# One-token attention and mixer layers on one core: query products spread over four row groups of PSUM, and unread products in the tail's pauses

## The chip, the core and the metric

The kernel runs on one core of a Trainium2 chip. The metric is device time in microseconds of one execution, lower is better. Engines are named as in the profile: PE is TensorE (its weight loads are listed apart as PEld), DVE is VectorE, ACT is ScalarE, POOL is GpSimd, and SP is the engine whose queue issues nearly all DMA transfers.

## The reference

Two requests (B = 2), each with one new token of width D = 512, go through four blocks: attention, mixer, attention, mixer, with the same weights for both layers. Everything is float32.

```
x = x + attention(layernorm(x), k_cache, v_cache, wq, wo)
x = x + mixer(layernorm(x), w1, b1, w2, b2)
x = x + attention(layernorm(x), k_cache, v_cache, wq, wo)
x = x + mixer(layernorm(x), w1, b1, w2, b2)

attention: 32 query heads of 128, 8 cache heads (4 query heads share one),
           32768 cached positions; softmax(q k^T / sqrt(128)) v, then @ wo
mixer:     u = gelu_tanh(h * w1 + b1)  (512 channels x 1792 hidden), y = u @ w2 + b2
```

Each layer has to read both caches (2 x 8 x 32768 x 128 values each), and layer 1's query needs the whole of layer 0. Some parts of the caches that layer 0 has read last are kept in SBUF for layer 1.

## The kernel before

**Units and steps.** The work is cut into 32 *units* (layer, request b, cache head h). A unit has 64 K cells and 64 V cells; a cell is 128 partitions x 512 floats (256 KB). `Order` writes out by hand one list of *steps*, each of four cells of one unit's K or V; the list sets the order of everything. A K step (`k_step`, L330) multiplies four cells by the unit's query into four different groups of 32 partitions of one PSUM bank. A V step (`v_step`, L383) multiplies four cells by the exponentials, also into four partition groups, of `acc`. Units alternate: the K of the next unit, then the V of this one. Steps 992 to 1007 are the V of the last unit but one, 1008 to 1023 the V of the last unit, whose last eight cells (a "thin" block, L392) use smaller products into a tile of `rows`.

**Memory and loads.** `mem` holds 106 cells. `plan_loads` goes through the steps in order and decides for each load its size, its place in `mem`, and after which step it is released, which is the last step that uses the cells it overwrites. To choose among places and sizes it keeps an estimate of when the DMA queue and TensorE are where; what a step's hooks cost TensorE comes from the `us=` figures given to `at`, summed in `busy`. SP issues the loads in that order (L790), each waiting until its cells are free.

**Hooks.** All other work is attached to steps with `at(step, function, ...)` and runs right after that step in program order:

- `make_q` makes queries, for both requests at once where it can. Its parts are hooked at three steps: two of the four products of `xn` (normalised input, 128 x 4 parts x 2 requests) with `wq` (L293), the other two and a copy to a row in SBUF (L298), and four small products that turn the row into columns (L302), which `q_out` copies into `qz` (L316).
- `take_out` copies `acc` (L414), `out_sum`/`out_1` add up its parts (L422), `out_2` applies `wo` (L446) and accumulates in `rows`.
- At the end of layer 0 of a request, `mix_1`, `mix_2`, `half_way` and `hidden_tiles` (L502, L517) compute the mixer while the V of a *filling* unit of the other request goes on, four cells a load. Then `change_1` and `change_2` make layer 1's first query: `columns` turns the mixer's output into four columns (L546), L558 adds the residual to give the new `x`, and L562 multiplies the raw `x`, and a column of ones beside it, by `wq` while mean and variance are found with `all_sum` (L540); the two results are combined with `pair` (L581).
- For the last unit, `last_rows` and `last_mixer` compute the last mixer with nothing left to load: sums (L422, L432), `wo` (L619), the row spread over all partitions (L628), statistics, fourteen hidden tiles on ScalarE (L662, L673) and their products (L652), and the store (L680).

The four accumulating products of a query (L293, L562) all write the same one or two PSUM rows:

```
for d in range(step * DT // 2, (step + 1) * DT // 2):
    nc.tensor.matmul(
        q_ps[us][:n, :], xn[layer][:, d, b : b + n], wq[:, d, :], start=(d == 0), stop=(d == DT - 1)
    )
```

Of the kernel before, what the change touches and what calls it, by code (L numbers as in the profile page):

```python
# [8 lines left out]
F32 = mybir.dt.float32  # L9
AF = mybir.ActivationFunctionType  # L10
ALU = mybir.AluOpType
# [184 lines left out]
def gqa_mixer_kernel(ctx: ExitStack, tc: tile.TileContext, x, kt, v, wqo, cols, out):  # L196
# [39 lines left out]
    acc = pfix.tile([P, G], F32, name="acc")  # L236
    rows = [pfix.tile([P, G], F32, name=f"rows{b}") for b in range(B)]
    S = [const.tile([P, G], F32, name=f"S{k}") for k in range(2)]
    xn = [const.tile([P, DT, B], F32, name=f"xn{k}") for k in range(2)]
    xq = [const.tile([P, DT, 2], F32, name=f"xq{b}") for b in range(B)]  # L240
    xT = {}

    def constants():
        make_identity(nc, ident)
        nc.gpsimd.memset(one, 1.0)
        nc.gpsimd.memset(half_neg, -0.5)
        nc.gpsimd.memset(qz, 0.0)
        for t in xq:
            nc.gpsimd.memset(t, 1.0)
        nc.vector.tensor_reduce(  # L250
            selg, ident.rearrange("p (g r) -> p r g", g=NG)[:, : R * QT, :], axis=AX.X, op=ALU.add
        )
        nc.vector.memset(acc, 0.0)
        for t in rows:
            nc.vector.memset(t, 0.0)

    def first_input():
        cen = work.tile([P, B, DT], F32, name="cen", bufs=1)
        sq = work.tile([P, B, DT], F32, name="sq", bufs=1)
        m = work.tile([P, B], F32, name="x_m", bufs=1)  # L260
        rs = work.tile([P, B], F32, name="x_rs", bufs=1)
        p = pmisc.tile([P, G], F32, name="misc")
        nc.tensor.matmul(p[:, : B * DT], ones, xcols.rearrange("p b d -> p (b d)"), start=True, stop=True)
        nc.vector.tensor_reduce(m, p[:, : B * DT].rearrange("p (b d) -> p b d", b=B), axis=AX.X, op=ALU.add)
        nc.vector.tensor_scalar_mul(m, m, 1.0 / D)
        for b in range(B):
            nc.vector.tensor_scalar_sub(cen[:, b, :], xcols[:, b, :], m[:, b : b + 1])
        nc.vector.tensor_mul(sq, cen, cen)
        p = pmisc.tile([P, G], F32, name="misc")
        nc.tensor.matmul(p[:, : B * DT], ones, sq.rearrange("p b d -> p (b d)"), start=True, stop=True)  # L270
        nc.vector.tensor_reduce(rs, p[:, : B * DT].rearrange("p (b d) -> p b d", b=B), axis=AX.X, op=ALU.add)
        nc.vector.tensor_scalar(rs, rs, 1.0 / D, EPS, op0=ALU.mult, op1=ALU.add)
        nc.gpsimd.tensor_tensor(rs, rs, half_neg.to_broadcast([P, B]), op=ALU.pow)
        for b in range(B):
            xT[b] = xcols[:, b, :]
            nc.vector.tensor_scalar_mul(xn[0][:, :, b], cen[:, b, :], rs[:, b : b + 1])

    def row_tile():
        return work.tile([P, D], F32, name="row", bufs=1)
# [4 lines left out]
    def make_q(us, step):  # L284

        layer, b, h = us[0]
        n = len(us)
        wq = wq_sb[layer, h] if (layer, h) in wq_sb else wq_sb[0, h]
        if step == 0:
            q_ps[us] = pmisc.tile([P, G], F32, name="misc")  # L290
        if step < 2:
            for d in range(step * DT // 2, (step + 1) * DT // 2):
                nc.tensor.matmul(  # L293
                    q_ps[us][:n, :], xn[layer][:, d, b : b + n], wq[:, d, :], start=(d == 0), stop=(d == DT - 1)
                )
        if step == 1:
            q_row[us] = row_tile()
            nc.vector.tensor_copy(q_row[us][:n, :], q_ps[us][:n, :])  # L298
        if step == 2:
            pt = pmisc.tile([P, G], F32, name="misc")  # L300
            for r in range(R):
                nc.tensor.matmul(  # L302
                    pt[:, r * n : (r + 1) * n],
                    q_row[us][:n, r * DH : (r + 1) * DH],
                    ident[:n, :n],
                    start=True,
                    stop=True,
                )
            q_out(us, pt)

    def q_out(us, pt):
        n = len(us)
        for j, u in enumerate(us):
            q_at[u] = 28 + 32 * (turn[0] % SLOTS)
            turn[0] += 1
            nc.vector.tensor_copy(  # L316
                qz[:, q_at[u] : q_at[u] + R], pt[:, : n * R].rearrange("p (r b) -> p b r", b=n)[:, j, :]
            )
# [214 lines left out]
    negm = const.tile([P, 1], F32, name="negm")  # L533
    spread = const.tile([P, 1], F32, name="spread")
    sq = const.tile([P, DT], F32, name="sq")
    pair = const.tile([2, 1], F32, name="pair")

    def all_sum(dst, src):
        p = pmisc.tile([P, G], F32, name="misc")
# [13 lines left out]

    def change_1(key, y):
        b = key[1]
        x = xq[b][:, :, 0]
        wq = wq_sb[0, y[2]]
        nc.vector.tensor_add(x, columns(key), sq)  # L558
        xT[b] = x
        q_ps[y] = pfix.tile([P, G], F32, name="bcast")  # L560
        for d in range(DT):
            nc.tensor.matmul(q_ps[y][:2, :], xq[b][:, d, :], wq[:, d, :], start=(d == 0), stop=(d == DT - 1))  # L562
        all_sum(negm, x)
        nc.vector.tensor_scalar_mul(negm, negm, -1.0 / D)
        nc.vector.tensor_scalar_add(xn[1][:, :, b], x, negm)
        nc.vector.tensor_mul(sq, xn[1][:, :, b], xn[1][:, :, b])
        q_row[y] = row_tile()
        nc.scalar.activation(q_row[y][:2, :], q_ps[y][:2, :], AF.Copy)

    def change_2(key, y):  # L570
        b = key[1]
        all_sum(spread, sq)
        nc.vector.tensor_scalar(spread, spread, 1.0 / D, EPS, op0=ALU.mult, op1=ALU.add)
        nc.gpsimd.tensor_tensor(spread, spread, half_neg, op=ALU.pow)
        nc.vector.scalar_tensor_tensor(
            pair, ident[:2, 1:2], negm[:2, :], ident[:2, 0:1], op0=ALU.mult, op1=ALU.add
        )
        nc.vector.tensor_scalar_mul(pair, pair, spread[:2, :])
        pt = pmisc.tile([P, G], F32, name="misc")
        for r in range(R):  # L580
            nc.tensor.matmul(  # L581
                pt[:, r : r + 1], q_row[y][:2, r * DH : (r + 1) * DH], pair, start=True, stop=True
            )
        q_out((y,), pt)
        nc.vector.tensor_scalar_mul(xn[1][:, :, b], xn[1][:, :, b], spread)

    rest = [None, None]

    def last_rows(u):
        layer, b, h = u  # L590
# [13 lines left out]
    def last_mixer(u):  # L604
# [12 lines left out]
        for k in range(2):  # L617
            for r in range(R):
                nc.tensor.matmul(  # L619
                    rest[k][32 * r : 32 * r + 1, :w],  # L620
                    oT[u][:, r : r + 1],
                    wo_of(u)[:, r, k * w : (k + 1) * w],
                    start=True,
                    stop=True,
                )
        nc.vector.tensor_copy(y[:, :w], rest[0][:, :w])
        nc.scalar.activation(y[:, w:], rest[1][:, :w], AF.Copy)
        nc.tensor.matmul(p, sel1, y, start=False, stop=True, skip_group_check=True)  # L628
# [2 lines left out]
        for g in range(NG):  # L631
            nc.tensor.matmul(
                rows[b][32 * g : 32 * g + 1, :P],
                selg[:, 0:1],
                y[:, g * P : (g + 1) * P],
                start=False,
                stop=False,
                skip_group_check=True,
            )
        nc.vector.bn_aggr(mv, st)  # L640
        deviation(rs, mv)
        off = work.tile([P, 1], F32, name="off", bufs=1)
# [18 lines left out]
        for f in range(DIRECT):  # L661
            nc.scalar.activation(  # L662
                tiles[f], flat, AF.Gelu_apprx_tanh, bias=bias[:, f : f + 1], scale=scale[:, f : f + 1]
            )
            project_last(f)
        f0 = DIRECT
        for m in TAIL_GROUPS:
            for f in range(f0, f0 + m):
                nc.vector.tensor_scalar(
                    tiles[f], flat, scale[:, f : f + 1], bias[:, f : f + 1], op0=ALU.mult, op1=ALU.add  # L670
                )
            t = cells(tail_at + f0, m)
            nc.scalar.activation(t, t, AF.Gelu_apprx_tanh)  # L673
            for f in range(f0, f0 + m):
                project_last(f)
            f0 += m
        assert f0 == FT
        o = tiles[FT][:, :P]
# [7 lines left out]
        busy[p] = busy.get(p, 0.0) + us  # L686

    def queries(us, p0, p1, p2):
        at(p0, make_q, us, 0, us=1.3)
        at(p1, make_q, us, 1, us=1.3)  # L690
        at(p2, make_q, us, 2, us=1.0)

    changed = {y: (x, fill) for x, fill, y in order.changes}
    opening = order.units[0]
# [21 lines left out]
    for u in order.units:  # L716
# [18 lines left out]
        if u == order.last:  # L735
            at(v0 - 1, take_rows, key)
            at(v0 - 1, table, AF.Gelu_apprx_tanh)
            at(v0 - 1, mix_1, key)
            at(v0 - 1, last_rows, u)
            at(v_end - 2, take_out, u)  # L740
            at(v_end - 1, out_sum, u)
            at(v_end, last_mixer, u)
            continue
# [21 lines left out]
            at(e + 1, mix_4, key, us=1.2)  # L765
            continue
        (y,) = [y for y, (x, _) in changed.items() if x == u]
        at(e + 1, change_1, key, y, us=2.8)
        at(e + 2, change_2, key, y, us=0.8)
        assert e + 2 < first["K", y]  # L770

# [85 lines left out]
```

## Time and profile before

| | |
|---|---|
| median of 3 runs | 2518.88 us (2519.59, 2512.27, 2518.88) |
| the profiled execution: time / span | 2518.04 / 2516.3 us |
| busy: PE, PEld, DVE, ACT, POOL | 1430.8, 400.0, 181.2, 186.2, 5.0 us |
| HBM read | 1064.33 MB, 423 GB/s over the span |
| mean granted PE clock | 0.754 |

Instructions are listed by the line that records them. A matmul in float32 shows as two records, and a group of them as one row with a count. "idle <-X" is the time for which the engine waited before them, and what ended that wait. The clock column of a window is the share of full TensorE speed that was granted; the DMA share is the mean over the core's 16 DMA engines. In a timeline, a row is start, duration, engine, line, operation, tiles, count; rows of equal kind may be merged, so a row's duration can hold waits inside it.

### The profile page before, as it was taken

The numbers are of one execution on the slowest core, as the hardware profiler recorded it, in microseconds if no ns is written. First come the engines' busy times: TensorE is split into PE (matmuls) and PEld (weight loads), VectorE is DVE, ScalarE is ACT, GpSimd is POOL, SyncE is SP. The second block draws the span as 40 slices with busy tenths as digits, with TensorE's granted clock in tenths as the row PEclk, the third lists the DMA queues.
The fourth block names the chain that finished last, engine by engine and source line by source line (L and its number), as shares of the span: only waits on it lengthen the run. The fifth ranks groups of instructions, "written<-read, shape, count | busy, mean of one in ns | idle before, by whom it ended". The sixth has DMA issues, their size and how long they took to land.

```text
span 2516.3 us, 20894 instructions
## 1 busy us (share of the span) xinstructions
PE 1430.8 (57%) x9550; PEld 400.0 (16%) x9550; DVE 181.2 (7%) x484; ACT 186.2 (7%) x580; POOL 5.0 (0%) x18
## 2 busy tenths in 40 slices
PE   4455555655556555547775775465555545565567
PEld 1111111111111111111121121111111111111112
DVE  1000000000000000000100010000000000000011
ACT  0100000000000000001111101000000000000021
POOL 0000000000000000000000000000000000000000
PEclk8777777777767777877898887677776776777787
DMA  9999999999999999999999999999999999999995
GB/s 417 429 432 432 431 433 433 433 431 434 427 433 430 434 431 432 417 434 421 390 425 425 394 423 438 433 431 434 433 432 432 431 432 427 434 434 433 432 426 238
DMA packets 32641, 1065.68 MB, mean 424 GB/s; under 512 B 3877, under 2 KB 3881, under 8 KB 5034
## 3 DMA queue, kind: packets, MB, share of 16 engines
q1 hardware_dynamic: 32264, 1064.32, 98.6%
q8 instruction: 75, 1.23, 0.2%
q14 instruction: 12, 0.10, 0.0%
q10 hardware_dynamic: 290, 0.03, 0.0%
HBM read 1064.33 MB, written 0.00 MB: 423 GB/s over the span
## 4 chain that ended last, share of the span: by engine, by line
DMA 73%; PE 26%; issue 0%; ACT 0%; DVE 0%; POOL 0%; SPq 0%; POOLq 0%
DMA mem<-in_kt_dram 37%; DMA mem<-in_v_dram 36%; PE acc L383 11%; PE scores L330 11%; PE misc L293 1%; PE misc L302 1%; PE misc L406 0%; PE bcast L562 0%; PE rows L502 0%; PE misc L422 0%; PE rows L652 0%; ACT S L365 0%; PE rows L392 0%; ACT mem L662 0%; PE bcast L628 0%
## 5 line engine op out<-in xcount | busy, mean ns | idle before, releaser
L330 PE MATMUL scores<-mem,qz 128*32 128x512 f32 x4096 | 619.4, 742 | 524.9 <-DMA mem<-in_kt_dram 524.9
L383 PE MATMUL acc<-mem,S 128*16 128x512 f32 x4080 | 600.3, 696 | 525.8 <-DMA mem<-in_v_dram 520.9
L365 ACT ACTIVATE S<-S,neg 128x128 f32<-128x128 f32 x256 | 129.8, 510 | 2237.7 <-DVE S L360 1214.9
L330 PEld LDWEIGHTS scores<-mem,qz 128*32 128x32 f32 x4096 | 140.9, 130 | 935.7 <-issue 471.1
L383 PEld LDWEIGHTS acc<-mem,S 128*16 128x16 f32 x4080 | 124.9, 104 | 839.8 <-issue 766.0
L340 DVE TENSOR_REDUCE mx<-scores 128x1 f32<-128x512 f32 x64 | 44.3, 692 | 840.7 <-PE scores L330 840.7
L293 PE MATMUL misc<-mem,xn 128*2 128x512 f32 (+1 forms) x128 | 74.2, 712 | 1.8 <-issue 1.8
L422 PEld LDWEIGHTS misc<-selg,row 128*128 128x128 f32 x256 | 48.9, 285 | 48.2 <-issue 36.8
L360 DVE STREAM_TRANSPOSE S<-scores 128x512 f32<-128x512 f32 x64 | 45.5, 711 | 123.3 <-PE acc L383 123.3
L422 PE MATMUL misc<-selg,row 128*128 128x4 f32 x256 | 51.7, 325 | 3.3 <-DVE row L414 3.3
L446 PE MATMUL rows<-mem,oT 128*1 128x512 f32 x248 | 52.5, 934 | 0.3 <-DVE oT L437 0.3
L365 ACT ACTIVATION_READ_ACCUMULATOR S<-S,neg 128x1 f32 x256 | 47.7, 186 | 0.0
L350 DVE TENSOR_REDUCE m<-misc 1x4 f32<-1x128 f32 x32 | 8.9, 279 | 363.3 <-PE misc L348 363.3
L414 DVE COPY row<-acc 128x512 f32<-128x512 f32 x32 | 22.1, 692 | 174.4 <-PE acc L383 174.4
L437 DVE TENSOR_TENSOR oT<-misc,rl 128x4 f32<-128x4 f32 x32 | 5.2, 163 | 257.1 <-PE misc L422 256.4
L298 DVE COPY row<-misc 2x512 f32<-2x512 f32 (+1 forms) x16 | 10.9, 679 | 170.0 <-PE misc L293 109.5
L293 PEld LDWEIGHTS misc<-mem,xn 128*2 128x2 f32 (+1 forms) x128 | 12.9, 101 | 63.4 <-issue 62.8
L502 PE MATMUL rows<-row,cols_sb 128*1 128x512 f32 x42 | 22.3, 614 | 0.6 <-ACT row L517 0.6
L502 PE MATMUL rows<-hid,cols_sb 128*1 128x512 f32 x42 | 22.3, 613 | 0.0
L408 DVE RECIPROCAL rl<-misc 128x4 f32<-128x4 f32 x32 | 5.9, 183 | 226.5 <-PE misc L406 226.5
L517 ACT ACTIVATE row<-bcast,bias,scale 128x512 f32<-128x512 f32 x21 | 16.3, 777 | 39.0 <-PE rows L502 20.2
L406 PEld LDWEIGHTS misc<-both,one 128*128 128x128 f32 x64 | 11.9, 232 | 40.5 <-issue 25.9
(115 smaller groups left out, 257.0 us busy)
## 6 DMA issues: line engine op xcount, KB each, us to landing
mem<-in_kt_dram SPq DMA_DIRECT2D x25, 2048.0 KB, 12.5
mem<-in_v_dram SPq DMA_DIRECT2D x37, 1024.0 KB, 8.8
mem<-in_wqo_dram SPq DMA_DIRECT2D x14, 2048.0 KB, 34.0
mem<-in_kt_dram SPq DMA_DIRECT2D x7, 4096.0 KB, 27.0
mem<-in_v_dram SPq DMA_DIRECT2D x7, 4096.0 KB, 17.6
mem<-in_kt_dram SPq DMA_DIRECT2D x18, 1024.0 KB, 9.9
mem<-in_v_dram SPq DMA_DIRECT2D x2, 6144.0 KB, 28.8
mem<-in_v_dram SPq DMA_DIRECT2D x5, 2048.0 KB, 10.6
```

The source lines that it names most:

```text
L293: nc.tensor.matmul(q_ps[us][:n, :], xn[layer][:, d, b : b + n], wq[:, d, :], start=(d == 0), stop=(d == DT - 1))
L302: nc.tensor.matmul(pt[:, r * n : (r + 1) * n], q_row[us][:n, r * DH : (r + 1) * DH], ident[:n, :n], start=True, stop=True,)
L330: nc.tensor.matmul(sc_ps[u, half][32 * row : 32 * row + 32, :], qz[:, at : at + 32], cells(at_cell["K", u, g], 1), start=(i == 0), stop=(i ...
L340: nc.vector.tensor_reduce(mx[u][:, half : half + 1], sc_ps[u, half], axis=AX.X, op=ALU.max)
L360: nc.vector.transpose(S[half], sc_ps[u, half])
L365: nc.scalar.activation(s[:, :, h], s[:, :, h], AF.Exp, bias=neg[u][:, h : h + 1], scale=SCALE, accum_out=lsum[u][:, half, h : h + 1],)
L383: nc.tensor.matmul(acc[32 * row : 32 * row + R * QT, :], S[half][:, col : col + R * QT], vc, start=(g < NG), stop=(g >= quads - NG),)
L414: nc.vector.tensor_copy(asb[u], acc)
L422: nc.tensor.matmul(po_of[u][:, :R], asb[u][:, t * DH : (t + 1) * DH], selg[:, t * R : (t + 1) * R], start=(t == 0), stop=(t == QT - 1 and ...
L446: nc.tensor.matmul(rows[b][32 * r : 32 * r + 1, :], oT[u][:, r : r + 1], wo_of(u)[:, r, :], start=(u == order.first_of[layer, b]), stop=(u ...
L502: nc.tensor.matmul(rows[key[1]][32 * g : 32 * g + 1, :], w2c[:, f : f + 1], hid.pop((key, f)), start=(f < NG), stop=(f >= FT - NG),)
L517: nc.scalar.activation(hid[key, f], px[key], AF.Gelu_apprx_tanh, bias=shift[key][:, f : f + 1], scale=slope[key][:, f : f + 1],)
```

## The change

1. The query products. `xn` and `xq` become one tile `xw` of 128 x 4 parts x 32 columns: columns 0 and 1 hold the normalised inputs of the two requests, column 2 the raw `x` of a layer change, column 3 ones, the rest zeros. `wide_products` multiplies each of the four parts into its own group of 32 partitions (start and stop in each), in place of accumulating four products in the same rows. `narrow_products` turns the row into columns as before, but contracts over all 128 partitions, with a selector (`selg`, ones at partitions r, 32 + r, 64 + r, 96 + r) or with `pair` as the moving side, so that it also adds up the four parts. All four products now come at the first of the three hooks.
2. A layer change uses the same two functions; its product lies in a buffer of `pmisc` and no longer in `bcast`. `x` is copied to a tile of its own, since column 2 of `xw` is used again.
3. `unread` multiplies a 128 x 1 vector of ones with `S[0]`, of 512 (G) or 128 (P) columns, into a tile that nothing reads. Such products are placed in the last unit's V steps and in `last_mixer`.
4. The figures for the planner: a query 1.1, 0 and 1.1 in place of 1.3, 1.3 and 1.0, `change_1` 2.2 in place of 2.8.
5. `dynamic_dma_scratch_size` is 512 in place of 1024; the kernel issues no DMA from POOL.

```
-    xn = [const.tile([P, DT, B], F32, name=f"xn{k}") for k in range(2)]
-    xq = [const.tile([P, DT, 2], F32, name=f"xq{b}") for b in range(B)]
+    xw = const.tile([P, DT, 32], F32, name="xw")
+    RAW = B
...
         if step == 0:
-            q_ps[us] = pmisc.tile([P, G], F32, name="misc")
-        if step < 2:
-            for d in range(step * DT // 2, (step + 1) * DT // 2):
-                nc.tensor.matmul(
-                    q_ps[us][:n, :], xn[layer][:, d, b : b + n], wq[:, d, :], start=(d == 0), stop=(d == DT - 1)
-                )
+            wide_products(us, wq_sb[layer, h] if (layer, h) in wq_sb else wq_sb[0, h])
         if step == 1:
             q_row[us] = row_tile()
-            nc.vector.tensor_copy(q_row[us][:n, :], q_ps[us][:n, :])
+            nc.vector.tensor_copy(q_row[us], q_ps[us])
         if step == 2:
-            pt = pmisc.tile([P, G], F32, name="misc")
-            for r in range(R):
-                nc.tensor.matmul(
-                    pt[:, r * n : (r + 1) * n], q_row[us][:n, r * DH : (r + 1) * DH], ident[:n, :n], ...
-            q_out(us, pt)
+            q_out(us, narrow_products(us, selg[:, b : b + n]))
+
+    def wide_products(us, wq):
+        q_ps[us] = pmisc.tile([P, G], F32, name="misc")
+        for d in range(DT):
+            nc.tensor.matmul(q_ps[us][32 * d : 32 * d + 32, :], xw[:, d, :], wq[:, d, :], start=True, stop=True)
+
+    def narrow_products(us, side):
+        n = side.shape[1]
+        pt = pmisc.tile([P, G], F32, name="misc")
+        for r in range(R):
+            nc.tensor.matmul(
+                pt[:, r * n : (r + 1) * n], q_row[us][:, r * DH : (r + 1) * DH], side, start=True, stop=True
+            )
+        return pt
...
     def change_1(key, y):
-        x = xq[b][:, :, 0]
-        nc.vector.tensor_add(x, columns(key), sq)
-        xT[b] = x
-        q_ps[y] = pfix.tile([P, G], F32, name="bcast")
-        for d in range(DT):
-            nc.tensor.matmul(q_ps[y][:2, :], xq[b][:, d, :], wq[:, d, :], start=(d == 0), stop=(d == DT - 1))
+        x = xw[:, :, RAW]
+        xT[b] = const.tile([P, DT], F32, name=f"xT_{b}")
+        pt = columns(key)
+        nc.vector.tensor_add(x, pt, sq)
+        wide_products(us, wq_sb[0, y[2]])
         all_sum(negm, x)
         nc.vector.tensor_scalar_mul(negm, negm, -1.0 / D)
-        nc.vector.tensor_scalar_add(xn[1][:, :, b], x, negm)
-        nc.vector.tensor_mul(sq, xn[1][:, :, b], xn[1][:, :, b])
-        q_row[y] = row_tile()
-        nc.scalar.activation(q_row[y][:2, :], q_ps[y][:2, :], AF.Copy)
+        nc.vector.tensor_scalar_add(cent, x, negm)
+        nc.vector.tensor_copy(xT[b], x)
+        nc.vector.tensor_mul(sq, cent, cent)
+        q_row[us] = row_tile()
+        nc.scalar.activation(q_row[us], q_ps[us], AF.Copy)
...
+    def unread(n, count=1):
+        if not idle:
+            idle.append(pmisc.tile([P, G], F32, name="misc"))
+        for _ in range(count):
+            nc.tensor.matmul(idle[0][:1, :n], one, S[0][:, :n], start=True, stop=True)
...
     def last_mixer(u):
...
+        unread(P)                      # after the wo products (L628 in the new numbering)
...
+        unread(G, 2)                   # after the row's own products, ahead of the statistics
...
             project_last(f)
+            unread(P)                  # after each of the first three hidden tiles
...
+            if m == max(TAIL_GROUPS):
+                unread(P)              # after each group of three hidden tiles
...
     def queries(us, p0, p1, p2):
-        at(p0, make_q, us, 0, us=1.3)
-        at(p1, make_q, us, 1, us=1.3)
-        at(p2, make_q, us, 2, us=1.0)
+        at(p0, make_q, us, 0, us=1.1)
+        at(p1, make_q, us, 1)
+        at(p2, make_q, us, 2, us=1.1)
...
+            at(v_mid, unread, G, 3)
+            at(v_mid + 4, unread, P, 2)
             at(v_end - 2, take_out, u)
+            at(v_end - 2, unread, G)
...
-        at(e + 1, change_1, key, y, us=2.8)
+        at(e + 1, change_1, key, y, us=2.2)
```

For the last unit, `v_mid` is step 1015 and `v_end` step 1023. In the new numbering L293 and L562 are L300, L302 and L581 are L307, L546 is L552, L558 is L566, L628 is L638, and the unread products are L596.

More of the change, by code (lines that the diff above doesn't have):

```diff
@@ L247, in constants @@
         nc.gpsimd.memset(qz, 0.0)
-        for t in xq:
-            nc.gpsimd.memset(t, 1.0)
+        nc.gpsimd.memset(xw, 0.0)
+        nc.gpsimd.memset(xw[:, :, RAW + 1], 1.0)
         nc.vector.tensor_reduce(
@@ L275, in first_input @@
             xT[b] = xcols[:, b, :]
-            nc.vector.tensor_scalar_mul(xn[0][:, :, b], cen[:, b, :], rs[:, b : b + 1])
+            nc.vector.tensor_scalar_mul(xw[:, :, b], cen[:, b, :], rs[:, b : b + 1])
     def row_tile():
@@ L287, in make_q @@
         n = len(us)
-        wq = wq_sb[layer, h] if (layer, h) in wq_sb else wq_sb[0, h]
         if step == 0:
-            q_ps[us] = pmisc.tile([P, G], F32, name="misc")
-        if step < 2:
-            for d in range(step * DT // 2, (step + 1) * DT // 2):
-                nc.tensor.matmul(
-                    q_ps[us][:n, :], xn[layer][:, d, b : b + n], wq[:, d, :], start=(d == 0), stop=(d == DT - 1)
-                )
+            wide_products(us, wq_sb[layer, h] if (layer, h) in wq_sb else wq_sb[0, h])
         if step == 1:
             q_row[us] = row_tile()
-            nc.vector.tensor_copy(q_row[us][:n, :], q_ps[us][:n, :])
+            nc.vector.tensor_copy(q_row[us], q_ps[us])
         if step == 2:
-            pt = pmisc.tile([P, G], F32, name="misc")
-            for r in range(R):
-                nc.tensor.matmul(
[L303 to L308, printed above, removed]
-            q_out(us, pt)
+            q_out(us, narrow_products(us, selg[:, b : b + n]))
[8 more added lines that the diff above has]
+            nc.tensor.matmul(
+                pt[:, r * n : (r + 1) * n],
+                q_row[us][:, r * DH : (r + 1) * DH],
+                side,
+                start=True,
+                stop=True,
+            )
+        return pt
     def q_out(us, pt):
@@ L535, in gqa_mixer_kernel @@
     sq = const.tile([P, DT], F32, name="sq")
-    pair = const.tile([2, 1], F32, name="pair")
+    cent = const.tile([P, DT], F32, name="cent")
+    pair = const.tile([P, 1], F32, name="pair")
     def all_sum(dst, src):
@@ L555, in change_1 @@
         b = key[1]
-        x = xq[b][:, :, 0]
-        wq = wq_sb[0, y[2]]
-        nc.vector.tensor_add(x, columns(key), sq)
-        xT[b] = x
-        q_ps[y] = pfix.tile([P, G], F32, name="bcast")
-        for d in range(DT):
-            nc.tensor.matmul(q_ps[y][:2, :], xq[b][:, d, :], wq[:, d, :], start=(d == 0), stop=(d == DT - 1))
+        us = (y,)
+        x = xw[:, :, RAW]
[3 more added lines that the diff above has]
+        wide_products(us, wq_sb[0, y[2]])
         all_sum(negm, x)
         nc.vector.tensor_scalar_mul(negm, negm, -1.0 / D)
-        nc.vector.tensor_scalar_add(xn[1][:, :, b], x, negm)
-        nc.vector.tensor_mul(sq, xn[1][:, :, b], xn[1][:, :, b])
-        q_row[y] = row_tile()
-        nc.scalar.activation(q_row[y][:2, :], q_ps[y][:2, :], AF.Copy)
+        nc.vector.tensor_scalar_add(cent, x, negm)
[3 more added lines that the diff above has]
+        nc.scalar.activation(q_row[us], q_ps[us], AF.Copy)
     def change_2(key, y):
@@ L575, in change_2 @@
         nc.vector.scalar_tensor_tensor(
-            pair, ident[:2, 1:2], negm[:2, :], ident[:2, 0:1], op0=ALU.mult, op1=ALU.add
+            pair, selg[:, RAW + 1 : RAW + 2], negm, selg[:, RAW : RAW + 1], op0=ALU.mult, op1=ALU.add
         )
[L578 to L585, printed above, removed]
-    rest = [None, None]
+        nc.vector.tensor_scalar_mul(pair, pair, spread)
+        q_out((y,), narrow_products((y,), pair))
+        nc.vector.tensor_scalar_mul(xw[:, :, b], cent, spread)
+    rest = [None, None]
+    idle = []
+    def unread(n, count=1):
[3 more added lines that the diff above has]
+            nc.tensor.matmul(idle[0][:1, :n], one, S[0][:, :n], start=True, stop=True)
     def last_rows(u):
@@ L842 @@
     given = _layout(*(np.asarray(a) for a in (A_x, A_k_cache, A_v_cache, A_wq, A_wo, B_w1, B_b1, B_w2, B_b2)))
-    nc = bacc.Bacc("TRN2", target_bir_lowering=False, num_devices=1, dynamic_dma_scratch_size=1024)
+    nc = bacc.Bacc("TRN2", target_bir_lowering=False, num_devices=1, dynamic_dma_scratch_size=512)
     arrays, args = {}, []
```

## The prediction

> **What bounds the kernel now.** The page comes first: its span, its DMA row and the chain that ended last.
>
> ```profile
> span 2516.3 us, 20894 instructions
> ...
> DMA  9999999999999999999999999999999999999995
> ...
> DMA 73%; PE 26%; issue 0%; ACT 0%; DVE 0%; POOL 0%; SPq 0%; POOLq 0%
> ...
> L293 PE MATMUL misc<-mem,xn 128*2 128x512 f32 (+1 forms) x128 | 74.2, 712 | 1.8 <-issue 1.8
> ...
> L437 DVE TENSOR_TENSOR oT<-misc,rl 128x4 f32<-128x4 f32 x32 | 5.2, 163 | 257.1 <-PE misc L422 256.4
> ```
>
> The DMA engines are busy in 39 of 40 slices, and the chain is DMA for 73%. So the kernel streams its caches, and a change can only win where the DMA engines run dry, or behind the last landing. The waits say what TensorE does meanwhile:
>
> ```profile
> PE scores L330 <- DMA mem<-in_kt_dram: 524.9, 79, 17.7
> ...
> PE acc L383 <- DMA mem<-in_v_dram: 520.9, 75, 16.8
> ```
>
> TensorE waits over 1000 us for loads. The windows view, cut fine, finds the dry places (the last two columns are the DMA share and GB/s):
>
> ```profile
> 1211.00:1218.00 7.00, 5.59 (x38) 2.24 (x42) 1.64 (x10) 0.53 (x1) 0.55 (x1) 0.81 0.52 176
> 1408.00:1414.00 6.00, 4.59 (x46) 2.12 (x42) 1.25 (x8) 0.00 (x0) 0.54 (x1) 1.00 0.57 198
> 2457.00:2462.00 5.00, 5.00 (x45) 1.27 (x49) 0.18 (x1) 0.00 (x0) 0.00 (x0) 0.93 0.64 242
> 2485.00:2496.00 11.00, 9.30 (x108) 3.88 (x104) 0.69 (x1) 0.00 (x0) 0.00 (x0) 0.81 0.65 234
> ```
>
> Lost DMA time is the missing share times the length: 7 x 0.48 = 3.4 us and 6 x 0.43 = 2.6 us at the two layer changes, 5 x 0.36 = 1.8 us and 11 x 0.35 = 3.9 us among the last loads. About 21 us of pure tail follow the last landing. These places are all there is to win.
>
> **Sixteen query products.** L293 has 128 records, eight to a product: four matmuls of two records each. They go one after the other now, side by side after the change; the prices stand below (3.52 us against 0.98), so 16 x 2.5 = 41 us of TensorE time go. Fourteen lie where TensorE waits for loads anyway, in the 1000 us above: nothing, and if that cover were gone the gain would be larger, not negative. Two lie in stretches where TensorE is behind, and there the DMA is full:
>
> ```profile
> 1280.00:1290.00 10.00, 10.00 (x73) 2.60 (x65) 1.99 (x3) 0.00 (x0) 0.00 (x0) 1.00 1.01 436
> 1460.00:1470.00 10.00, 10.00 (x70) 2.93 (x62) 0.93 (x3) 0.00 (x0) 0.00 (x0) 1.00 1.02 437
> ```
>
> Nothing there either. I count zero for all sixteen. The copy of 128 rows instead of two, and a turn that contracts 128 rows, are in the same cover.
>
> **The two layer changes.** Here TensorE must make the next layer's query before it goes on with the values whose cells the next loads need. TensorE's timeline, then the DMA queue's:
>
> ```profile
> 1204.94 1.05 PE L383 MATMUL acc<-mem,S 128*16 128x512 f32 x8 [0.52 <-DMA mem<-in_v_dram]
> 1205.92 1.05 PE L546 MATMUL misc<-selg,row 128*128 128x1 f32 x8
> 1207.32 3.59 PE L562 MATMUL bcast<-mem,xq 128*2 128x512 f32 x8 [0.35 <-DVE xq L558]
> 1210.84 0.39 PE L540 MATMUL misc<-xq,one 128*128 128x4 f32 x2
> 1211.15 1.05 PE L383 MATMUL acc<-mem,S 128*16 128x512 f32 x8
> 1212.22 0.36 PE L540 MATMUL misc<-sq,one 128*128 128x4 f32 x2
> ...
> 1214.92 4.46 PE L383 MATMUL acc<-mem,S 128*16 128x512 f32 x24
> ```
> ```profile
> 1206.05 0.33 SPq L790 DMA_DIRECT2D mem<-in_v_dram  x1
> 1212.27 4.62 SPq L790 DMA_DIRECT2D mem<-in_kt_dram  x2
> ```
>
> The serial product holds TensorE from 1207.32 to 1210.84, 3.52 us. Four matmuls of 512 columns into four row groups are in this trace: L383 starts at 1204.94 and the next instruction at 1205.92, 0.98 us. So the product gets 2.54 us shorter. Added to the path is one VectorE copy of 128x4 (the column, ahead of the squares): 0.16 us by L437, 0.2 with its step. The second sum takes the buffer the product used, so it now waits for ScalarE's copy; at 1208.3 plus some 0.7 us that is done before the sum, due at 1209.9. Behind all this queue the value steps at 1211.15 and 1214.92, and behind those the loads: SP issues nothing from 1206.05 until 1212.27, just after the step of 1211.15 ends, and its next load after the step of 1214.92. All come 2.54 - 0.2 = 2.35 us sooner. Both losses (3.4 and 2.6 us) exceed that, so all of it counts: **-4.7 us** for two. Bounds: -5.1 with the copy hidden, 0 with no overlap.
>
> The Trainium skill ("TensorE: Matmul & The Clock Gate", Part 3, measured speedups) gives 2.38 times for three column tiles. By that alone the four would take an estimated 3.52 / 2.38 = 1.5 us, and the two changes would gain 3.7 us. The L383 row, which is the same shape of work, says 0.98, and I follow it.
>
> **The last loads.** The added code does not name this part. The hooks' costs, which the load planner reads, fall (3.6 to 2.2 us a query, 2.8 to 2.2 us a change), and the planner picks other cells. I worked its list out for both kernels. Before, the last unit's eight value loads are released by steps 999, 1003, 1007, 1014, 1016, 1018, 1019 and 1019; after, by 999, 999, 1007 and five times 1011. Also the unit ahead loads its first 32 cells as 24 and 8, so TensorE can start them sooner. In the trace of before the releases are late:
>
> ```profile
> 2443.17 0.33 SPq L790 DMA_DIRECT2D mem<-in_v_dram  x1
> ...
> 2459.35 0.33 SPq L790 DMA_DIRECT2D mem<-in_v_dram  x1
> ...
> 2478.38 0.33 SPq L790 DMA_DIRECT2D mem<-in_v_dram  x1
> ```
> ```profile
> 2472.13 7.07 PE L383 MATMUL acc<-mem,S 128*16 128x512 f32 x64
> 2483.73 7.67 PE L383 MATMUL acc<-mem,S 128*16 128x512 f32 x48 [4.53 <-DMA mem<-in_v_dram]
> 2493.10 1.06 PE L392 MATMUL rows<-mem,S 128*4 128x128 f32 x32 [1.70 <-DMA mem<-in_v_dram]
> 2494.09 1.05 PE L422 MATMUL misc<-selg,row 128*128 128x4 f32 x8
> 2495.07 1.73 PE L392 MATMUL rows<-mem,S 128*4 128x128 f32 x32
> 2497.20 0.59 PE L432 MATMUL misc<-selg,mem 128*128 128x4 f32 x2 [0.40 <-DVE mem L614]
> 2498.04 1.89 PE L619 MATMUL scores<-mem,oT 128*1 128x256 f32 x16 [0.25 <-DVE oT L437]
> 2500.43 2.08 PE L628 MATMUL bcast<-mem,selg 128*128 128x512 f32 x2 [0.50 <-ACT mem L627]
> ```
>
> The load of 2459.35 is step 1003's and follows the hole that starts at 2457; released with the one of 2443.17, it has no hole. The load of 2478.38 is step 1014's. Steps 1008 to 1015 are the 32 matmuls from 2472.13, so step 1011 ends at 2475.7, and the five last loads are all queued then, long before the DMA is done with the one ahead (which L383 waits for until 2483.73). Both holes can close: 1.8 + 3.9 us, less the 0.9 us of that window behind the last landing (2495.07): 4.8 us, landing at 2490.3.
>
> TensorE must keep up, now with unread products in its way. A 512-column one costs 3.52 / 4 = 0.88 us at full clock, a 128-column one a quarter. L383 costs 7.07 / 32 = 0.22 a matmul. From 2479.20: three unread, 2481.8; 24 matmuls, 2487.1; two small and one wide unread, 2488.5; thin block 0.99, 2489.5; sums 0.98, 2490.5; second thin block 1.06, 2491.5. Before, that point is 2496.80: -5.3 us. At half clock throughout: three unread 5.3, the measured 7.67, then 0.9 + 1.8, 0.99, 0.98 and 1.73 give 2498.6, +1.8 us. I take **-4.5 us**, near the first end, since the unread products stand in the very pause after which the clock fell.
>
> **The clock in the tail.** The windows again, cut at its changes (the column ahead of the DMA share is the granted clock):
>
> ```profile
> 2488.50:2495.30 6.80, 5.10 (x78) 2.54 (x74) 0.69 (x1) 0.00 (x0) 0.00 (x0) 1.00 0.66 231
> 2495.30:2512.30 17.00, 12.14 (x152) 4.73 (x144) 8.15 (x21) 7.77 (x9) 0.55 (x1) 0.50 0.00 1
> 2512.30:2516.30 4.00, 0.77 (x28) 0.39 (x16) 0.35 (x1) 0.00 (x1) 0.00 (x0) 0.93 0.00 1
> ```
> ```profile
> 1180.30 1.12 PE L480 MATMUL bcast<-row,selg 128*128 128x512 f32 x2
> ```
>
> The same broadcast takes 1.12 us at full clock (L480) and 2.08 in the tail (L628), where the clock is 0.50. At that ratio, 0.54, the three products on the path (0.59 + 1.89 + 2.08 = 4.56) lose 2.1 us. The rest of the tail is ScalarE's:
>
> ```profile
> 2504.92 2.23 ACT L662 ACTIVATE mem<-mem,bias,scale 128x512 f32<-128x512 f32 x3 [4.54 <-DVE bias L648]
> 2507.05 5.25 ACT L673 ACTIVATE mem<-mem 128x1536 f32<-128x1536 f32 x5
> ```
>
> From 2504.92 to 2512.30 it is never idle, and the unread products there run in its shadow, for nothing; if the clock stays at half, they push TensorE past ScalarE by up to 1 us. I take **-1.8 us** of a range from +1 to -2.1.
>
> The Trainium skill (same page, table of two states in Part 1) has the clock fall after an idle window of about 3.4 us. Here it fell at 2495.3 after a stretch with 5.10 of 6.80 us busy, so a pause shorter than that is enough.
>
> **Sum.** -4.7 - 4.5 - 1.8 = -11.0 us. The profiled execution took 2518.04 us, 1.7 beyond its span; 2507.0 after. The median of the runs is 0.84 above that execution: 2507.9, so 2508.
>
> **Rivals.**
> *The products do not overlap.* Then the changes stay as they are and only the tail gains: 2518.9 - 6.3 = 2512.6. Against it: L383 does overlap. 0.10.
> *TensorE becomes the bound of the tail.* The clock falls in spite of the unread products, and their own time eats what the loads win: +1.8 and +1 in place of -4.5 and -1.8, with the changes' -4.7: 2517.0; half of that, 2512.5. For it: one-column products may count little as activity. Against: after the one-column products at the end of the tail the clock came back (0.93 in the last window). 0.22.
> *Slower: loads released later.* In the stretches of 1280 and 1460, where TensorE has no idle time, the new list releases six loads one or two steps later (525 for 523, 528 for 527, 600 for 599, 627 for 625, 635 for 634, 647 for 646). That is eight steps in all. A step is four matmuls, 0.88 us at full clock, twice that at half: 14 us if the queue holds nothing else, and each time it runs dry it restarts at a price like the hole of 2457, 1.8 us, 11 us for six. 2508 becomes 2533. It decides once it passes 11 us. Against: the DMA share there is 1.01, at full clock, so the queue is not empty. 0.07.
> *The forecast*, with its terms within their bounds (2503 to 2512): 0.61.
>
> **Numbers.** About 0.3%, 7.6 us, is what a measurement of this kernel can tell from no change; faster means below 2511.3. The forecast gives 0.56 of its 0.61, the partial tail some 0.07: 0.63. Slower 0.07. Same 0.30. The range reaches from all bounds reached, 2502, to the partial rivals, 2516.
>
> **What would show it.** Right: in the windows at the two changes the DMA share rises and the gap from the last columns product to the next value step shrinks by about 2.3 us; the last two loads' holes are closed, and the last landing is about 5 us nearer to the end of the layer changes; L638 takes about 1.1 us and the tail's clock is 1.00. Wrong: the wide product takes over 3 us; the granted clock is still 0.50 when L638 runs; new dips in the DMA row between 1290 and 1540; or the thin blocks start late because TensorE still works off unread products.

## The result and the profile after

The changed kernel takes 2509.52 us (median of 12 runs, 2505.99 to 2512.67), the kernel before 2516.55 us on the same chip (12 runs, 2512.27 to 2519.59). The ratio is 0.9974, 95% interval 0.9965 to 0.9982: 6.5 us faster, outside the interval of no change, and by a little less than the 0.3% that the prediction had named as its bound (the median is below the 2511.3 us that it gave for that, since the kernel before has come down too). The profiled execution of the changed kernel is its slowest, 2512.67 us with a span of 2511.0. Executions of one kernel scatter by 2.7 us (standard deviation over all the runs of this document), more than most single parts of this change turn out to be worth, so one pair of profiles shows mechanisms, and only the runs show sizes.

The page of the changed kernel: span, the DMA row of the slices, and the group of the sixteen query products and the two changes' products.

```profile
span 2511.0 us, 20944 instructions
...
DMA  9999999999999999999999999999999999999996
...
L300 PE MATMUL misc<-mem,xw 128*32 128x512 f32 x144 | 19.7, 619 | 2.4 <-DVE xw L276 1.9
```

The waits of the changed kernel (engine, line, what it waited for; us in total, times, longest):

```profile
PE scores L335 <- DMA mem<-in_kt_dram: 553.2, 82, 17.8
PE acc L388 <- DMA mem<-in_v_dram: 529.4, 75, 16.5
```

TensorE is busy 38.7 us less (1392.1 us for 1430.8), and it waits 36.8 us longer for loads (553.2 + 529.4 for 524.9 + 520.9). What TensorE saved, most of it on the sixteen products, went into waiting, as forecast.

The first layer change, TensorE's timeline and the DMA queue's in the changed kernel:

```profile
1205.05 1.05 PE L388 MATMUL acc<-mem,S 128*16 128x512 f32 x8 [0.50 <-DMA mem<-in_v_dram]
1206.04 1.05 PE L552 MATMUL misc<-selg,row 128*128 128x1 f32 x8
1207.35 1.06 PE L300 MATMUL misc<-mem,xw 128*32 128x512 f32 x8 [0.26 <-DVE xw L566]
1208.34 0.38 PE L546 MATMUL misc<-xw,one 128*128 128x4 f32 x2
1208.66 1.05 PE L388 MATMUL acc<-mem,S 128*16 128x512 f32 x8
1209.64 0.39 PE L546 MATMUL misc<-sq,one 128*128 128x4 f32 x2
...
1212.51 4.27 PE L388 MATMUL acc<-mem,S 128*16 128x512 f32 x24
```
```profile
1209.77 10.34 SPq L807 DMA_DIRECT2D mem<-in_kt_dram  x6
```

The product holds TensorE from 1207.35 to 1208.34, 0.99 us where it was 3.52 (L300 here for L562 before). The value step that stood at 1211.15 stands at 1208.66, the one of 1214.92 at 1212.51, and SP's first load behind the change is issued at 1209.77 instead of 1212.27. Everything is 2.4 to 2.5 us sooner. In the second change the wide product starts at 1404.63 and the last value step at 1409.67, 5.04 us later; before it was 7.60 us, from 1403.60 to 1411.20.

The end, in the changed kernel: TensorE's timeline, then windows.

```profile
2483.25 3.63 PE L388 MATMUL acc<-mem,S 128*16 128x512 f32 x32 [1.28 <-DMA mem<-in_v_dram]
2486.68 0.60 PE L596 MATMUL misc<-S,one 128*1 128x128 f32 x4
2488.08 1.91 PE L388 MATMUL acc<-mem,S 128*16 128x512 f32 x16 [0.80 <-DMA mem<-in_v_dram]
2489.80 1.02 PE L596 MATMUL misc<-S,one 128*1 128x512 f32 x2
2490.53 1.17 PE L397 MATMUL rows<-mem,S 128*4 128x128 f32 x32
...
2494.72 1.04 PE L628 MATMUL scores<-mem,oT 128*1 128x256 f32 x16 [0.26 <-DVE oT L442]
2495.59 0.38 PE L596 MATMUL misc<-S,one 128*1 128x128 f32 x2
2496.27 1.12 PE L638 MATMUL bcast<-mem,selg 128*128 128x512 f32 x2 [0.30 <-ACT mem L637]
```
```profile
2457.00:2462.00 5.00, 5.00 (x44) 1.18 (x48) 0.18 (x1) 0.00 (x0) 0.00 (x0) 0.90 1.00 433
2495.30:2511.00 15.70, 9.15 (x152) 4.11 (x140) 8.05 (x20) 7.77 (x9) 0.54 (x1) 1.00 0.01 1
```

The hole of 2457 is gone (share 1.00 where it was 0.64), the clock is 1.00 through the tail where it was 0.50, and L638 takes 1.12 us where L628 took 2.08. Of the signs that the prediction named, the shorter changes, the full clock and the shorter L638 are there. Two are not. The second hole is not closed: the 11 us around the end of the loads, 2485 to 2496 before, lie from 2482.3 to 2493.3 now if they are laid by the start of the last transfer, and the DMA share in them is 0.65 as it was. And the last landing is not about 5 us nearer to the end of the layer changes: the last transfer begins 1082.9 us after the value step at 1409.67, where it began 1084.0 us after the one at 1411.20, which is 1.1 us nearer.

### The profile page after: what moved, and what is told of

It is laid out like the page before. It is cut to its first block, busy times and chain, and to the rows that moved or that the text cites. A ratio compares the mean times of both kernels' runs of the same rounds, so it can differ in the third digit from the quotient of the medians.

```text
span 2511.0 us, 20944 instructions
## 1 busy us (share of the span) xinstructions
PE 1392.1 (55%) x9580; PEld 395.3 (16%) x9580; DVE 179.7 (7%) x486; ACT 186.2 (7%) x580; POOL 5.1 (0%) x18
## 5 line engine op out<-in xcount | busy, mean ns | idle before, releaser
L335 PE MATMUL scores<-mem,qz 128*32 128x512 f32 x4096 | 614.6, 740 | 553.2 <-DMA mem<-in_kt_dram 553.2
L388 PE MATMUL acc<-mem,S 128*16 128x512 f32 x4080 | 591.4, 713 | 534.4 <-DMA mem<-in_v_dram 529.4
L427 PEld LDWEIGHTS misc<-selg,row 128*128 128x128 f32 x256 | 48.9, 285 | 48.2 <-issue 36.8
L300 PE MATMUL misc<-mem,xw 128*32 128x512 f32 x144 | 19.7, 619 | 2.4 <-DVE xw L276 1.9
L307 PEld LDWEIGHTS misc<-selg,row 128*128 128x128 f32 x128 | 16.3, 199 | 17.7 <-issue 10.1
L307 PE MATMUL misc<-selg,row 128*128 128x2 f32 (+1 forms) x128 | 17.7, 260 | 0.8 <-DVE row L292 0.8
```

The costliest lines, as they stand in the source:

```text
L300: nc.tensor.matmul(q_ps[us][32 * d : 32 * d + 32, :], xw[:, d, :], wq[:, d, :], start=True, stop=True)
L307: nc.tensor.matmul(pt[:, r * n : (r + 1) * n], q_row[us][:, r * DH : (r + 1) * DH], side, start=True, stop=True,)
L335: nc.tensor.matmul(sc_ps[u, half][32 * row : 32 * row + 32, :], qz[:, at : at + 32], cells(at_cell["K", u, g], 1), start=(i == 0), stop=(i ...
L388: nc.tensor.matmul(acc[32 * row : 32 * row + R * QT, :], S[half][:, col : col + R * QT], vc, start=(g < NG), stop=(g >= quads - NG),)
L427: nc.tensor.matmul(po_of[u][:, :R], asb[u][:, t * DH : (t + 1) * DH], selg[:, t * R : (t + 1) * R], start=(t == 0), stop=(t == QT - 1 and ...
```

## The experiments

In this pair of profiles the bytes moved by the changed kernel lead those of the kernel before by about 1.4 us' worth after the first change, and the lead is back at zero at 1260 us and again at 1540. So the first theory (A in the expectations that give it a letter) was that the changes' lead is lost again behind them. Its rival: the changes keep their gain, and the tail's terms were too large. The first four runs take the change apart. "Between the means" is the difference of the two kernels' mean times.

**Products alone.** The changed kernel with all four old figures for the planner and without any call of `unread`:

```
-        at(p0, make_q, us, 0, us=1.1)
+        at(p0, make_q, us, 0, us=1.3)
...
-            unread(P)
...
```

> The kernel after with the planner's old figures (so the old list of loads) and without the unread products: the new query products alone. Theory A (the layer changes' lead is given back within the next 60 us, as the two profiles show): 0 to -1.5 us against before, although the gap from the first columns product to the next value step is 2.4 us shorter. Theory B (the prediction: each change's 2.35 us lasts): -4.7 us.

Measured: 2510.13 us (8 runs), ratio 0.9975 (0.9964 to 0.9987) to the kernel before at 2515.84 (27 runs, shared by the four): -5.6 us between the means. Theory A falls: the products alone bring more than the 4.7 us forecast for the two changes.

**Figures alone.** The kernel before with the four new figures:

> The kernel before with only the three planner figures of the change (the new list of loads, old products, no unread products). Theory A: this is where the last loads' gain comes from, -2 to -4 us at the last thin block, the hole at 2457 closed, with 20 us of tail behind it as before. Theory B: -4.5 us. Rival C (the plan needs the faster products to pay): 0 or slower, since the planner now takes TensorE for faster than it is.

Measured: 2514.34 us (12 runs), 0.9991 (0.9981 to 1.0): -2.0 us between the means, at the edge of what can be told from nothing, and less than half of 4.5, though the interval, which reaches to -4.8 us, does not exclude that by itself.

**Unread products alone.** The kernel before with `unread` and its calls:

> The kernel before with only the unread products. Theory A and B: the tail behind the last thin block shrinks by 1.8 to 2.2 us, with a granted clock of 1.00 in it; -2 us in all, as the last landings stay where they were. Rival D (unread products in front of the thin blocks cost what they win): 0.

Measured: 2514.29 us (12 runs), 0.9989 (0.9978 to 1.0): -1.8 us, again at the edge.

**The change without unread products.**

> The kernel after without the unread products. Theory A: the loads' part remains, the clock's goes: -3 us against before, tail behind the last thin block 19.5 us again. Theory B: -9.2 us. Rival D: -5 us or more, as fast as after.

Measured: 2510.09 us (8 runs), 0.997 (0.9959 to 0.9982): -6.8 us between the means, as much as the whole change.

The list of loads now brought about 1 to 2 us instead of 4.5. Either it costs something elsewhere (it also differs in the middle, between 1280 and 1540 us: theory M), or its gain in the tail is simply small (theory O). Two runs split the list, one undoes the changes' gain, and one puts together the version that theory M would make the best.

**The new list for the tail only.** Products alone, and for the hooks from step 610 on the new figures (the other two hooks of a query likewise):

```
-        at(p0, make_q, us, 0, us=1.3)
+        old = p0 < 610
+        at(p0, make_q, us, 0, us=1.3 if old else 1.1)
...
```

> Column group products as in the changed kernel, no unread products; the planner's new figures only for the list of the tail, so that the order of loads up to 1280 us and through the middle is the one before the change, and the last sixteen are released as in the changed kernel. Theory M (the new list costs 2 to 3 us in the middle, between 1280 and 1540 us, and that hides what it gains in the tail): -8.5 us against the kernel before. Theory O (the list's gain in the tail is only about 1 us and nothing is lost in the middle; the parts overlap): -6.8 us, like the changed kernel without its unread products.

Measured: 2510.95 us (11 runs), 0.9979 (0.9968 to 0.9989) to 2515.49 (32 runs, shared by these four): -5.0 us between the means. Theory M wanted -8.5, outside the interval (-2.8 to -8.0).

**The new list for the middle only.** The same with `p0 >= 610`, and `change_1` at 2.2:

> The reverse: products, no unread, the new figures only for the list of the middle, the tail's loads released as before the change. Theory M: -3 us against the kernel before, 2 to 3 us behind the products alone. Theory O: -5.6 us, like the products alone.

Measured: 2510.06 us (11 runs), 0.9986 (0.9977 to 0.9994): -4.8 us between the means. No loss in the middle that could hide 2 to 3 us is seen, though the interval (-1.5 to -5.8) holds both theories.

**The changes lengthened again.** Products alone, with three serial products put into the change:

```
         wide_products(us, wq_sb[0, y[2]])
+        late = pfix.tile([P, G], F32, name="bcast")
+        for d in range(3):
+            nc.tensor.matmul(late[:2, :], xw[:, 0, :2], wq_sb[0, y[2]][:, d, :], start=(d == 0), stop=(d == 2))
```

> Products alone, as in the run of the products alone, but in the first layer change three serial products of 512 columns (about 2.6 us) are added right behind the column group product, so that the change is as long as before. If the gain of the products lies in the layer changes, half of it goes: about -3 us against the kernel before (the second change keeps its share). If it lies in the sixteen other query products or the tail, -5.6 us stays. If the helper is run in both changes, the whole gain goes: 0 to -1 us.

The helper runs in both changes, so the last case holds. In this kernel's timeline of TensorE the added products are L570, and the value step that ends the first change comes 8.39 us after the start of the wide product (7.60 before, 5.16 in the changed kernel). So each change is not only as long as before but 0.8 us longer:

```profile
1205.63 1.06 PE L300 MATMUL misc<-mem,xw 128*32 128x512 f32 x8 [0.26 <-DVE xw L566]
1206.51 2.74 PE L570 MATMUL bcast<-mem,xw 128*2 128x512 f32 x6
...
1214.02 5.21 PE L388 MATMUL acc<-mem,S 128*16 128x512 f32 x24
```

Measured: 2516.78 us (11 runs), 1.0003 (0.9994 to 1.0013): the whole gain of the products is gone, +0.2 us between the means. With 0.8 us too much in each of the two changes, up to 1.6 us of a gain elsewhere could hide behind that. The windows around the two changes say the same (the last two columns are DMA share and GB/s). The kernel before, this one, the products alone, and the changed kernel:

```profile
1180.00:1235.00 55.00, 45.50 (x268) 12.37 (x268) 5.94 (x25) 14.06 (x21) 1.09 (x2) 0.85 0.95 388
1380.00:1435.00 55.00, 40.35 (x254) 9.99 (x250) 5.52 (x21) 12.21 (x17) 0.79 (x2) 0.90 0.96 397
```
```profile
1180.00:1235.00 55.00, 43.41 (x270) 12.41 (x272) 6.19 (x26) 13.31 (x19) 1.08 (x2) 0.89 0.94 384
1380.00:1435.00 55.00, 46.55 (x286) 13.10 (x278) 6.05 (x25) 15.10 (x25) 1.08 (x2) 0.87 0.92 365
```
```profile
1180.00:1235.00 55.00, 41.68 (x276) 11.41 (x268) 6.75 (x27) 14.30 (x22) 1.09 (x2) 0.90 1.00 409
1380.00:1435.00 55.00, 38.96 (x270) 9.98 (x258) 5.58 (x22) 12.21 (x17) 0.58 (x2) 0.91 0.99 405
```
```profile
1180.00:1235.00 55.00, 43.98 (x269) 11.74 (x268) 6.67 (x26) 13.71 (x20) 1.09 (x2) 0.84 0.98 397
1380.00:1435.00 55.00, 40.16 (x263) 10.28 (x262) 6.38 (x26) 12.38 (x18) 1.08 (x2) 0.87 0.99 400
```

Lost DMA time, 55 us times the missing shares of both windows: 5.0, 7.7, 0.6 and 1.7 us. In the other profiles the two kernels with long changes (figures alone, unread products alone) lose 8.8 and 6.1 us in these windows, and the six with short ones 0.6 to 2.2 us. So it is 5 to 9 us with the long changes and about 2 at most with the short ones.

**Tail list and unread products.** The version that theory M would make 3 us faster than the changed kernel:

> Products, the tail's new list alone, and the unread products. Theory M: -10 us against the kernel before, that is 3 us faster than the changed kernel. Theory O: -7 us, like the changed kernel. The thin block's tail, from the last copy of the accumulator of the last but one unit on, to the store is about 45 us in both.

Measured: 2509.27 us (10 runs), 0.9972 (0.9961 to 0.9982): as fast as the changed kernel, not faster. Theory M is out. No version run here beats the changed kernel by anything that can be measured.

**The list alone, on top of everything else.** The changed kernel with the old figures, and beside it the changed kernel itself:

> The changed kernel with the planner's old figures: column group products and unread products, the old list of loads. Against the next run, the changed kernel itself on the same chip, the difference is the whole list alone, with everything else as in the change. The prediction's term for the last loads: this one 4.5 us longer than the changed kernel. A fit of all runs so far with additive parts: 1.3 us longer (bounds 0 to 2.6), and about 6 us shorter than the kernel before. Overlap of list and unread products: no difference.

> The changed kernel itself, for the comparison on the same chip: by the fit -7.4 us against the kernel before; if list and unread products overlap, -6 us. Its last transfers drain over 3 to 4 us at a falling share, as in its first profile, where the old list ends with short holes and then stops at once.

Measured: 2510.06 us (8 runs), 0.9975 (0.9965 to 0.9986), and 2509.2 us (8 runs), 0.9975 (0.9964 to 0.9985), to the kernel before at 2515.18 (15 runs). Between the means the list is worth 1.0 us. The profiles show why so little. The last 4 us before the last landing and the time from 2450 to there, in the kernel with the old list:

```profile
2450.00:2487.00 37.00, 31.97 (x224) 10.50 (x228) 3.12 (x9) 3.62 (x10) 0.00 (x0) 0.82 0.96 402
2487.00:2491.00 4.00, 4.00 (x66) 2.40 (x62) 0.69 (x1) 0.00 (x0) 0.00 (x0) 1.00 0.65 250
```

and with the new list (the changed kernel's second profile):

```profile
2450.00:2486.85 36.85, 30.95 (x224) 10.89 (x228) 3.13 (x9) 3.60 (x10) 0.00 (x0) 0.83 0.98 416
2486.85:2490.85 4.00, 4.00 (x58) 2.19 (x54) 0.69 (x1) 0.00 (x0) 0.00 (x0) 1.00 0.37 142
```

Old list: 37 x 0.04 + 4 x 0.35 = 2.9 us lost. New list: 36.85 x 0.02 + 4 x 0.63 = 3.3 us. The holes ahead are closed, and the same time is lost at the very end, where the last transfers drain at a falling share. The changed kernel's first profile has it too:

```profile
2450.00:2488.60 38.60, 31.45 (x224) 10.46 (x228) 3.13 (x9) 3.61 (x10) 0.00 (x0) 0.81 0.97 415
2488.60:2492.60 4.00, 4.00 (x58) 2.07 (x50) 0.69 (x1) 0.00 (x0) 0.00 (x0) 1.00 0.28 108
```

The other traces bear this out. In the 5 us where the first hole stood (5.8 to 0.8 us ahead of the copy of the last but one unit's accumulator, as in the kernel before), the DMA share is 0.64 to 0.76 in all six profiles with the old list in the tail and 0.97 to 1.05 in all six with the new one. Yet from 10 us ahead of that copy to the start of the last transfer the lost DMA time is 2.3 to 4.6 us with the old list (3.3 on average; the kernel before has the 4.6) and 2.4 to 3.4 with the new one (2.9 on average). Why the last transfers drain so slowly once all are queued early was not tried.

## Why the prediction was right, and where it was not

All 197 runs of the kernels above and of the kernel before, fitted by least squares with one number for each part (parts simply added, and one base for each group of runs on one chip), give sizes that a single comparison is too coarse for:

| part | predicted, us | fitted, us (95%) |
|---|---|---|
| products | -4.7 | -4.6 ± 1.1 |
| planner's list | -4.5 | -1.3 ± 1.2 (tail -1.0, middle -0.3, ± 1.2 each) |
| unread products | -1.8 | -1.3 ± 1.1 |
| three serial products put back into both changes | | +4.7 ± 1.9 |
| the whole change | -11.0 | -7.1 ± 1.2 |

No kernel's mean lies more than 0.7 us from the fit, so the parts need no interaction to explain the runs.

**The time itself: luck in part.** 2508 us were forecast and 2509.52 measured, but the forecast gain of 11.0 us is 3.9 above the fitted 7.1. The kernel before, 2518.88 us in the three runs that the prediction had, is 2516.55 in twelve, and these 2.3 us made up for more than half of the error. Nor does the lower end of the range, 2502, follow from the terms: their best bounds, -5.1, -5.3 and -2.1, add up to 2506.4 us.

**Right: the layer changes.** The step moved 2.4 us in one and 2.6 us in the other (2.35 forecast), and the loads behind it moved by about the same. Two such steps are 5.0 us, and the products are worth 4.6 ± 1.1, so the time followed about one for one where the DMA engines had been dry. That the gain sits in the changes is shown by the run that lengthens them again. The Trainium skill ("TensorE: Matmul & The Clock Gate", Part 3, measured speedups) gives 2.38 times for three column tiles. Here four went from 3.52 to 0.99 us, 3.6 times, and the measurement decides.

**Right: the sixteen products at nothing.** 38.7 us less TensorE work came back as 36.8 us more waiting for loads. The run with long changes bounds what is left of them: products and the serial products together give +0.1 ± 1.8 us in the fit. Since the changes are 1.6 us longer in it than in the kernel before, the sixteen products could still be worth 1.5 ± 1.8 us: nothing that can be told from zero, and far from the 41 us of TensorE time, but zero is not shown.

**Wrong in size: the last loads.** The step that failed is "both holes can close: 1.8 + 3.9 us, less 0.9". The first hole did close (0.64 to 1.00), and so it does in every profile with the new list. The second did not: the time won was lost again in the slow drain. And its price was read off one profile. In it the last transfer starts 32.5 us after the copy of the last but one unit's accumulator starts. In the five other profiles with the old list it starts 29.0 to 32.1 us after it, in the six with the new list 28.3 to 29.7. On average these are 30.6 and 29.3, so the new list wins 1.3 us there, close to the 1.0 ± 1.2 that the fit gives it in the tail, and the profile that was priced lay at the late end. Why the old list scatters so is open. The clock alone does not explain it: while the last 24 matmuls of 512 columns ran (x48 records), the kernel before had a mean clock of 0.69, the products alone 0.66 with the last transfer at 30.8 us, and the unread products alone 0.94 with 32.1 us. The prediction took a value near the better end of its range (-5.3 to +1.8); a value between the ends would have been right.

**Right by half: the clock in the tail.** The changed kernel's first profile does what was forecast, and the time from the end of the second thin block to the output's store is 14.46 us for 16.72. But the same kernel's second profile has the clock at 0.50 from 2493.18 to 2496.59, in spite of the unread products:

```profile
2492.87 1.64 PE L628 MATMUL scores<-mem,oT 128*1 128x256 f32 x16 [0.26 <-DVE oT L442]
2494.26 0.64 PE L596 MATMUL misc<-S,one 128*1 128x128 f32 x2
2494.99 1.91 PE L638 MATMUL bcast<-mem,selg 128*128 128x512 f32 x2
```

and a kernel without unread products (the list for the middle only) keeps the full clock there:

```profile
2491.97 1.04 PE L628 MATMUL scores<-mem,oT 128*1 128x256 f32 x16 [0.26 <-DVE oT L442]
2493.52 1.12 PE L637 MATMUL bcast<-mem,selg 128*128 128x512 f32 x2 [0.50 <-ACT mem L636]
```

Over the profiles, that stretch takes 14.46 to 15.82 us with unread products (five) and 14.41 to 16.72 without (seven), 15.0 and 15.4 on average. The broadcast of the row (L638 in the changed kernel) takes 1.12 us in three of the five profiles with unread products and in four of the seven without, so that they keep the clock up at that place is not shown. Over the whole stretch the mean clock is 0.89 to 1.00 with them and 0.54 to 0.77 without, but most of that is ScalarE's time. The kernel before's profile was again the worst of its kind.

**The rivals.** That the products do not overlap is refuted by the row of 0.99 us. That loads released later in the middle make it slower: the run with the new list there alone shows no loss, and the share from 1290 to 1540 is 1.00 (0.99 before). That TensorE becomes the bound of the tail: in the changed kernel the steps behind the pauses still wait for a load (1.28 and 0.80 us above), so the unread products ahead of them lie in real pauses. But its condition, that the clock falls in spite of the unread products, is met in two of the five profiles. And over the last 4 us of loading TensorE is busy without a pause (4.00 of 4.00 us in both profiles of the changed kernel), so whether a still earlier landing would be worth its full length there is not shown.

## What to carry to other kernels

In a kernel that streams, shorten the steps behind which the next loads are released, and price them one for one only where the DMA share shows that the engines run dry. A saving of TensorE time elsewhere, here 39 us, brought nothing that the runs can tell from zero. A hole or a slow clock that stands in one profile is one execution's: before it becomes a term of a sum, see in several profiles how far it scatters, and take the middle of its range if it does. And a hole that closes is worth its length only if the same time is not lost again further on.

## What was not expected of the hardware

With the last five loads all queued 12 us or more ahead of the start of the last transfer, the DMA engines did not end at full share. Over the last 4 us it was 0.28 to 0.50 in the six profiles with the new list. With the old one, where the last load is issued only 3.4 to 7.7 us ahead, it was 0.50 to 0.85 in six.

And the same instructions in the same tail met a full clock in one execution and half in the next. In the second profile of the changed kernel the slow stretch lasts 3.41 us, from 2493.18. In the 3.41 us ahead of it TensorE was busy 2.74 us. In the first profile it was busy 2.74 us of the 3.41 that end at 2495.58, and there the clock stayed at 1.00.
